# Full matmuls in column tiles, and the third phase of the VectorE exponential added by GpSimd

## The chip, the cores and the metric

The kernel runs on one core of one Trainium2 chip. The metric is the time of one execution in device microseconds (us). All executions of the kernel before lay between 801 and 824 us. They differ mainly in how long TensorE's clock was granted at half speed, which each run records as a mean granted clock. A run counts as slow when it is over 1.5% above the fastest of its kernel, and as fast otherwise.

## The reference, cut to what matters

```python
# S = 2048 tokens, D = 512, 32 heads of 16, F = 1792, all bfloat16
g = sigmoid((x * gate_w).sum(-1, keepdims=True))
a = softmax(q @ k.T * 16**-0.5) @ v  (per head), then @ wo
b = (sigmoid(x @ w_gate) * (x @ w_up)) @ w_down
return g * a + (1 - g) * b
```

The largest part is the exponential of 32 x 2048 x 2048 scores.

## The kernel before

The kernel contains a small scheduler. It describes each instruction as a task with an engine, a planned duration and its inputs, and lays out a fixed order per engine. On the chip each engine runs its order strictly and waits on semaphores. A wrong planned duration makes no wrong result, only an order that doesn't fit.

Scores are computed with keys on the partitions. There are 32 units (8 groups of four heads by 4 blocks of 512 queries), each with 16 key tiles. For twelve key tiles ScalarE computes the exponential. For the other four (1, 5, 9, 13) VectorE does it by a trick: a linear map of the score, written as a 16-bit integer, is the bit pattern of a float16 close to the exponential. Three such patterns, shifted by a third of an octave each and weighted, give a better one. The first shift ("phase") is the map from PSUM; the second and third add a constant to the first, SBUF to SBUF:

```python
PH_OFF = (0, 342, 683)
...
es.append(P.add("dve", 0.61, lambda v, b=b, bp=bp, i=i: v.tensor_scalar(
    PDu[:, bp.slot, 0, i, :], bk(b), EXP_A, EXP_B, op0=ALU.mult, op1=ALU.add), [t], [b, bp], kind="x", prio=1.0))
...
ph_ = [es]
for m in range(1, NPH):
    ph_.append([P.add("dve", 0.33, lambda v, bp=bp, m=m: v.tensor_scalar(
        PDu[:, bp.slot, m, :, :], PDu[:, bp.slot, 0, :, :], float(PH_OFF[m]), None, op0=ALU.add), es, [bp], kind="x")])
```

A block is two heads of one key tile: 1024 elements per partition. There are 256 blocks, and three buffers for them. TensorE works in three modes. Scores use row tiles (32 rows each). PV products (probabilities by values) use four column tiles of 17 columns. Everything else, here called full matmuls, uses the whole array. GpSimd prepares keys and queries and is idle most of the time.

```python
eK[g, r, c] = P.add("pool", 1.0, lambda p, r=r: p.tensor_scalar(
    K[:, g, r, c * 512:(c + 1) * 512], kraw[:, kr.slot, :], msk[:, r:r + 1], msk[:, 2 + r:3 + r],
    op0=ALU.mult, op1=ALU.add), [ev, e_msk], [kr], kind="m")
...
eVm[g, kt, m] = P.add("pool", 0.35, lambda p, i=i, kt=kt, m=m: p.tensor_scalar(
    Vm[:, m - 1, i, 8 * g:8 * g + 8, :], V[:, kt, 8 * g:8 * g + 8, :], PH_W[m], 1.0,
    op0=ALU.mult, op1=ALU.mult), [eV[g, t0], e_one], kind="m", prio=1)
```

## Time and profile before

| | before |
|---|---|
| time, two runs | 801.67 and 812.08 us |
| profiled run | span 817.3 us, mean granted clock 0.964 |
| TensorE, ScalarE, VectorE, GpSimd busy | 94%, 93%, 82%, 11% |

The profiled run was a slow one, with 61 us at half clock. The prediction shows the lines that carry the reading. Three more rows are GpSimd's in the groups of instructions. Columns: line, engine, operation, output and input with shapes and types, count; then busy us and the mean ns of one; then idle time before them.

```profile
L624 POOL TENSOR_SCALAR K<-un,msk 128x512 bf16<-128x512 bf16 x28 | 26.3, 947 | 10.3 <-ACT un L612 10.2
...
L668 POOL COPY Q<-Q 128x512 bf16<-128x512 bf16 x15 | 10.5, 699 | 0.0
L699 POOL TENSOR_SCALAR Vm<-V 128x136 bf16<-128x136 bf16 x32 | 9.9, 309 | 81.8 <-DVE V L695 53.5 <-DVE e2p L718 24.7 <-DVE a_ L636 2.5
```

### The profile page before, as it was taken

The numbers are of one execution on the slowest core, as the hardware profiler recorded it, in microseconds if no ns is written. First come the engines' busy times: TensorE is split into PE (matmuls) and PEld (weight loads), VectorE is DVE, ScalarE is ACT, GpSimd is POOL, SyncE is SP. The second block draws the span as 40 slices with busy tenths as digits, with TensorE's granted clock in tenths as the row PEclk, the third lists the DMA queues.
The fourth block names the chain that finished last, engine by engine and source line by source line (L and its number), as shares of the span: only waits on it lengthen the run. The fifth ranks groups of instructions, "written<-read, shape, count | busy, mean of one in ns | idle before, by whom it ended". The sixth has DMA issues, their size and how long they took to land.

```text
span 817.3 us, 15633 instructions
## 1 busy us (share of the span) xinstructions
PE 770.8 (94%) x6509; PEld 236.6 (29%) x6604; DVE 666.6 (82%) x1318; ACT 756.1 (93%) x838; POOL 88.2 (11%) x160
## 2 busy tenths in 40 slices
PE   7999999999999899999999999999999999999996
PEld 4323333232222222222222222222222222222222
DVE  4986999988988868877889877878988878878783
ACT  3787999989999989999999999999999999999990
POOL 4700523410100000000000001000000100000000
PEclk8975999989999979999999999999999999999998
DMA  9100000011000000000000000000000000000000
GB/s 325 63 2 2 1 2 1 2 57 36 2 1 2 2 1 1 14 8 8 1 2 2 1 1 14 8 8 2 1 1 2 2 14 8 7 1 1 2 1 26
DMA packets 10830, 12.92 MB, mean 16 GB/s; under 512 B 1680, under 2 KB 9736, under 8 KB 10760
## 3 DMA queue, kind: packets, MB, share of 16 engines
q1 hardware_dynamic: 8856, 10.48, 3.8%
q10 hardware_dynamic: 1904, 1.44, 0.5%
q8 instruction: 52, 0.85, 0.4%
q14 instruction: 18, 0.15, 0.1%
HBM read 9.70 MB, written 2.10 MB: 14 GB/s over the span
## 4 chain that ended last, share of the span: by engine, by line
PE 59%; ACT 31%; DVE 7%; issue 1%; DMA 1%; ACTq 0%
ACT PA L786 30%; PE ps_all L753 19%; PE ps_all L762 17%; PE ps_all L596 10%; PE ps_all L858 7%; DVE PD L802 3%; PE ps_all L863 2%; DVE PD L806 2%; PE ps_all L689 1%; ACT tT L730 1%; DMA PD<-in_A_x_dram 1%; PE ps_all L826 1%; PE ps_all L576 1%; PE ps_all L846 0%; DVE hT L733 0%
## 5 line engine op out<-in xcount | busy, mean ns | idle before, releaser
L786 ACT ACTIVATE PA<-ps_all 128x1024 bf16<-128x1024 f32 x768 | 729.4, 1061 | 31.2 <-PE ps_all L753 23.5
L802 DVE TENSOR_SCALAR PD<-ps_all 128x512 uint16<-128x512 f32 x512 | 345.7, 686 | 93.5 <-PE ps_all L753 81.2
L753 PE MATMUL ps_all<-Q,K 32*128 32x512 bf16 x2048 | 312.2, 394 | 22.6 <-ACT PA L786 16.0
L762 PE MATMUL ps_all<-PA,V 128*17 128x512 bf16 x1536 | 244.0, 393 | 0.1
L806 DVE TENSOR_SCALAR PD<-PD 128x1024 uint16<-128x1024 uint16 x512 | 206.7, 437 | 4.8
L762 PE MATMUL ps_all<-PD,Vm 128*17 128x512 f16 x1024 | 183.4, 396 | 1.5 <-issue 1.0
L753 PEld LDWEIGHTS ps_all<-Q,K 32*128 32x128 bf16 x2048 | 75.4, 91 | 274.4 <-ACT PA L786 219.1
L762 PE MATMUL ps_all<-PD,V 128*17 128x512 f16 x512 | 138.2, 394 | 1.1 <-DVE PD L802 0.7
L762 PEld LDWEIGHTS ps_all<-PA,V 128*17 128x17 bf16 x1536 | 51.6, 88 | 59.5 <-issue 50.9
L596 PE MATMUL ps_all<-xT,wu 128*128 128x512 bf16 x208 | 64.8, 388 | 1.5 <-issue 0.8
L596 PE MATMUL ps_all<-xT,wg 128*128 128x512 bf16 x194 | 63.1, 388 | 2.8 <-issue 1.9
L858 PE MATMUL ps_all<-un,hT 128*128 128x512 bf16 x200 | 60.1, 383 | 3.0 <-issue 2.1
L835 POOL TENSOR_TENSOR rs<-rec,e 128x16 f32<-128x16 f32 x32 | 8.0, 250 | 499.1 <-DVE rec L833 498.9
L762 PEld LDWEIGHTS ps_all<-PD,Vm 128*17 128x17 bf16 x1024 | 40.3, 89 | 37.5 <-issue 30.7
L733 DVE SCALAR_TENSOR_TENSOR hT<-tT,ps_all 128x512 bf16<-128x512 bf16 x56 | 38.2, 682 | 12.6 <-PE ps_all L596 12.4
L762 PEld LDWEIGHTS ps_all<-PD,V 128*17 128x17 bf16 x512 | 29.4, 88 | 24.5 <-issue 19.5
L730 ACT ACTIVATE tT<-ps_all 128x512 bf16<-128x512 f32 x56 | 35.5, 634 | 0.0
L666 POOL TENSOR_TENSOR qsq<-Q 128x512 bf16<-128x512 bf16 x15 | 16.5, 1098 | 106.5 <-DVE Q L665 106.5
L624 POOL TENSOR_SCALAR K<-un,msk 128x512 bf16<-128x512 bf16 x28 | 26.3, 947 | 10.3 <-ACT un L612 10.2
L596 PEld LDWEIGHTS ps_all<-xT,wg 128*128 128x128 bf16 x224 | 16.7, 97 | 35.6 <-issue 28.1
L596 PEld LDWEIGHTS ps_all<-xT,wu 128*128 128x128 bf16 x224 | 16.9, 97 | 33.8 <-issue 24.3
L858 PEld LDWEIGHTS ps_all<-un,hT 128*128 128x128 bf16 x224 | 16.9, 97 | 33.4 <-issue 24.8
(79 smaller groups left out, 354.2 us busy)
## 6 DMA issues: line engine op xcount, KB each, us to landing
wg<-in_B_w_gate_dram SPq DMA_DIRECT2D x1, 1792.0 KB, 11.9
wu<-in_B_w_up_dram SPq DMA_DIRECT2D x1, 1792.0 KB, 16.3
un<-in_B_w_down_dram SPq DMA_DIRECT2D x1, 1792.0 KB, 8.6
out_dram<-ost SPq DMA_DIRECT2D x14, 128.0 KB, 1.7
PD<-in_A_x_dram SPq DMA_DIRECT2D x4, 256.0 KB, 6.1
PD<-in_A_x_dram ACTq DMA_DIRECT2D x4, 256.0 KB, 6.9
un<-in_A_wqkv_dram SPq DMA_DIRECT2D x1, 512.0 KB, 8.8
wo<-in_A_wo_dram SPq DMA_DIRECT2D x1, 512.0 KB, 14.9
```

Of the source, the lines that this page charges most:

```text
L596: return lambda pe: pe.matmul(bk(b), w_ap(dt), x_ap(dt), start=(dt == 0), stop=(dt == 3))
L624: eK[g, r, c] = P.add("pool", 1.0, lambda p, r=r: p.tensor_scalar(K[:, g, r, c * 512:(c + 1) * 512], kraw[:, kr.slot, :], msk[:, r:r + 1], ...
L666: s = P.add("pool", 1.15, lambda p: p.tensor_tensor(qsq[:, sq.slot, :], Q[:, bq.slot, 0, :], Q[:, bq.slot, 0, :], ALU.mult), [ev], [sq, bq ...
L730: et = P.add("act", 0.48, lambda a: a.activation(tT[:, t_.slot, :], bk(b), ACTF.Tanh, scale=0.5), [l1], [b, t_], kind="m")
L733: e_h[c, ft] = P.add("dve", 0.62, lambda v: v.scalar_tensor_tensor(hT[:, h_.slot, :], tT[:, t_.slot, :], 1.0, bk(b2), ALU.add, ALU.mult), ...
L753: return pe.matmul(bk(b), K[32 * j:32 * j + 32, g, r, kt * 128:(kt + 1) * 128], Q[32 * j:32 * j + 32, bq.slot, r, :], start=True, stop=Tru ...
L762: return pe.matmul(bk(bpv)[32 * j:32 * j + DH + 1, :], lhs(h), rhs(), start=t.first, stop=t.last, tile_position=(0, 32 * j), skip_group_ch ...
L786: return a.activation(o, ps_all[:, lo:hi + 1:hi - lo, :], ACTF.Exp, bias=ACT_BIAS, scale=SCALE)
L802: es.append(P.add("dve", 0.61, lambda v, b=b, bp=bp, i=i: v.tensor_scalar(PDu[:, bp.slot, 0, i, :], bk(b), EXP_A, EXP_B, op0=ALU.mult, op1 ...
L806: ph_.append([P.add("dve", 0.33, lambda v, bp=bp, m=m: v.tensor_scalar(PDu[:, bp.slot, m, :, :], PDu[:, bp.slot, 0, :, :], float(PH_OFF[m] ...
L858: mms.append((MM, lambda pe, i=i, h_=h_, ft=ft: pe.matmul(bk(b), hT[:, h_.slot, sl], wd[:, ft, :], start=(i == 0), stop=(i == n - 1))))
L863: mms.append((MM, lambda pe, i=i, bs=bs, g=g: pe.matmul(bk(b), OTs[:, bs.slot, sl], wo[:, g, :], start=(i == 0), stop=(i == n - 1))))
```

## The change

The intent: VectorE, at 82%, gives one of three phases to the idle GpSimd. Full matmuls are issued as four column tiles, so that they share PV's mode and need no change of mode beside PV work. The issue rule waits for fuller score sets.

```diff
-N_A, N_D, N_F, N_DF, D_LAG, D_LEAD, N_C = 2, 2, 2, 3, 6, 3, 2
+N_A, N_D, N_F, N_DF, D_LAG, D_LEAD, N_C = 3, 2, 2, 3, 6, 3, 2
+EARLY, LATE = 1.6, 0.9
...
+                if lead < LATE or two or (len(ds) == 2 and lead < EARLY):
+                    if two and not (len(ds) == 2):
+                        s.append(q)
...
-        self._issue([t], now, "F", [[t]])
+        if t.alt:
+            t.emit = t.alt
+        self._issue([t], now, "C" if t.alt else "F", [[t]])
...
+    def full(b, w, x, first, last):
+
+        def four(pe):
+            for j in range(4):
+                i = pe.matmul(bk(b)[32 * j:32 * j + 32, :], w()[:, 32 * j:32 * j + 32], x(), start=first, stop=last,
+                              tile_position=(0, 32 * j), skip_group_check=True)
+            return i
...
-                        ph_.append([P.add("dve", 0.33, lambda v, bp=bp, m=m: v.tensor_scalar(
+                        ph_.append([P.add(*(("pool", 1.45) if m == 2 else ("dve", 0.33)), lambda v, bp=bp, m=m: v.tensor_scalar(
```

More of the change, by code (lines that the diff above doesn't have):

```diff
@@ L82, in pair, with pairs2 @@
         return next((i for i in range(7) if i in at and i + 1 in at), None)
+    def pairs2(self):
+        at = {i for _, i, _ in self.free}
+        i = self.pair()
+        return i is not None and any(j in at and j + 1 in at for j in range(i + 2, 7))
     def take(self, buf, at=None):
@@ L96 @@
     __slots__ = ("eng", "dur", "emit", "deps", "bufs", "kind", "prio", "key", "lanes", "succ", "nd", "seq", "start",
-                 "vis", "ready", "dma", "nbytes", "group", "unit", "war", "known", "val", "n", "first", "last")
+                 "vis", "ready", "dma", "nbytes", "group", "unit", "war", "known", "val", "n", "first", "last", "alt")
     def __init__(self, eng, dur, emit, deps=(), bufs=(), kind="", prio=0.0, key=0.0, lanes=(), dma=False, nbytes=0, n=0):
@@ L106, in __init__ @@
         self.first = self.last = False
+        self.alt = None
 class Plan:
@@ L126, in group @@
         ts = []
-        for i, (dur, emit) in enumerate(mms):
+        for i, (dur, emit, *alt) in enumerate(mms):
             t = self.add("pe", dur, emit, deps if i == 0 else [ts[0]], ([bank] if bank else []) + list(bufs), kind="F", key=key)
+            t.alt = alt[0] if alt else None
             ts.append(t)
@@ L150, in run @@
         self.mode = None
+        self.inflight = []
         self.dma_free = 0.0
@@ L258, in _issue @@
         self.mode = mode
+        if mode == "R":
+            self.inflight = [x for x in self.inflight if x.vis > now] + [x for s in sets for x in s if x.kind == "R"]
         end = t0
@@ L276, in _pe @@
             if p.nd == 0 and ps.pair() is not None and nA < N_A and not (self.dbl and self.dbl[0].n < self.pi - D_LAG):
+                lead = self._lead(now)
                 s = [p]
-                self.pi += 1
-                self.prog = self.pi / len(self.pairs) * UNITS
                 lanes = set(p.lanes)
-                k = 0
-                while k < min(4, len(self.dbl)) and len(s) < 3:
+                q = self.pairs[self.pi + 1] if self.pi + 1 < len(self.pairs) else None
+                two = (q is not None and q.nd == 0 and nA + 2 <= N_A and not lanes & set(q.lanes) and ps.pairs2()
+                       and not (self.dbl and self.dbl[0].n < self.pi + 1 - D_LAG))
+                k, ds = 0, []
+                while k < min(4, len(self.dbl)) and len(ds) < 2:
                     d = self.dbl[k]
-                    if d.n > self.pi + (D_LEAD if len(s) == 1 else -1):
+                    if d.n > self.pi + 1 + (D_LEAD if len(ds) == 0 else -1):
                         break
-                    if (d.nd == 0 and nfree >= 2 + len(s) and nD + len(s) <= N_D and nD + nF + len(s) <= N_DF
+                    if (d.nd == 0 and nfree >= 3 + len(ds) and nD + len(ds) + 1 <= N_D and nD + nF + len(ds) + 1 <= N_DF
                             and d.lanes[0] not in lanes):
-                        s.append(d)
+                        ds.append(k)
                         lanes.add(d.lanes[0])
-                        self.dbl.pop(k)
-                    else:
-                        k += 1
-                return self._issue(s, now, "R", [s])
+                    k += 1
+                if lead < LATE or two or (len(ds) == 2 and lead < EARLY):
+                    if two and not (len(ds) == 2):
+                        s.append(q)
+                    else:
+                        s += [self.dbl[k] for k in ds]
+                        for k in reversed(ds):
+                            self.dbl.pop(k)
+                    self.pi += sum(x.kind == "R" for x in s)
+                    self.prog = self.pi / len(self.pairs) * UNITS
+                    return self._issue(s, now, "R", [s])
         behind = self.dbl and (self.pi >= len(self.pairs) or self.dbl[0].n < self.pi - D_LAG // 2)
@@ L314, in _pe, with _lead @@
         return False
+    def _lead(self, now):
+        x = max(0.0, self.freeat["act"] - now) + sum(t.dur for t in self.ready["act"] if not t.dma)
+        return x + sum(0.905 for t in self.inflight if t.vis > now)
     def _cset(self, now):
@@ L592, in xTd @@
         return [eT[c, 0], eT[c, 1]]
+    def full(b, w, x, first, last):
[4 more added lines that the diff above has]
+            return i
+        return (MM, lambda pe: pe.matmul(bk(b), w(), x(), start=first, stop=last), four)
     def mm4(b, w_ap, x_ap):
-        def one(dt):
-            return lambda pe: pe.matmul(bk(b), w_ap(dt), x_ap(dt), start=(dt == 0), stop=(dt == 3))
-        return [(MM, one(dt)) for dt in range(4)]
+        return [full(b, lambda dt=dt: w_ap(dt), lambda dt=dt: x_ap(dt), dt == 0, dt == 3) for dt in range(4)]
     def xq(c):
@@ L857, in final_mms @@
             h_ = b_h[c, ft]
-            mms.append((MM, lambda pe, i=i, h_=h_, ft=ft: pe.matmul(bk(b), hT[:, h_.slot, sl], wd[:, ft, :], start=(i == 0),
-                                                                    stop=(i == n - 1))))
+            mms.append(full(b, lambda h_=h_: hT[:, h_.slot, sl], lambda ft=ft: wd[:, ft, :], i == 0, i == n - 1))
         for i, g in enumerate(gs_):
@@ L862, in final_mms @@
             i = i + len(fts)
-            mms.append((MM, lambda pe, i=i, bs=bs, g=g: pe.matmul(bk(b), OTs[:, bs.slot, sl], wo[:, g, :], start=(i == 0),
-                                                                  stop=(i == n - 1))))
+            mms.append(full(b, lambda bs=bs: OTs[:, bs.slot, sl], lambda g=g: wo[:, g, :], i == 0, i == n - 1))
         return mms, [e_h[c, ft] for ft in fts] + [e_OTs[c, g] for g in gs_] + [ewo, e_wd], [b_h[c, ft] for ft in fts] + [b_OTs[c, g] for g in gs_]
```

## The prediction

> **What bounds the kernel now.** I read the page first (busy shares and chain), then the groups, the windows by stage, and timelines of ScalarE, TensorE and the VectorE/GpSimd pair.
>
> ```profile
> PE 770.8 (94%) x6509; PEld 236.6 (29%) x6604; DVE 666.6 (82%) x1318; ACT 756.1 (93%) x838; POOL 88.2 (11%) x160
> PE 59%; ACT 31%; DVE 7%; issue 1%; DMA 1%; ACTq 0%
> L786 ACT ACTIVATE PA<-ps_all 128x1024 bf16<-128x1024 f32 x768 | 729.4, 1061 | 31.2 <-PE ps_all L753 23.5
> L802 DVE TENSOR_SCALAR PD<-ps_all 128x512 uint16<-128x512 f32 x512 | 345.7, 686 | 93.5 <-PE ps_all L753 81.2
> L806 DVE TENSOR_SCALAR PD<-PD 128x1024 uint16<-128x1024 uint16 x512 | 206.7, 437 | 4.8
> ```
>
> Two engines are nearly full, and the chain alternates between them. ScalarE has a floor: where it isn't starved it starts an exponential every 0.915 us (a row of three took 2.85 us, a lone one 1.02). 768 of them are 703 us, and 56 tanh at 0.475 us between starts add 27, so 730 us. The first exponential starts at 25.8 us and the last ends at 799.0, so ScalarE loses some 43 us in those 773. The rest of the span, 26 us ahead and 18 us behind, is projections and final matmuls.
>
> TensorE's busy share says little, so I take starts. These rows are of the timeline of TensorE from 664 us on (start, duration, line, operation):
>
> ```profile
> 664.18 0.39 PE L762 MATMUL ps_all<-PD,Vm 128*17 128x512 f16 x1
> ...
> 664.63 0.38 PE L762 MATMUL ps_all<-PA,V 128*17 128x512 bf16 x1
> ...
> 664.94 0.39 PE L753 MATMUL ps_all<-Q,K 32*128 32x512 bf16 x3
> ...
> 665.80 0.39 PE L753 MATMUL ps_all<-Q,K 32*128 32x512 bf16 x3
> ...
> 666.13 0.82 PE L858 MATMUL ps_all<-un,hT 128*128 128x512 bf16 x3
> ...
> 666.88 0.39 PE L753 MATMUL ps_all<-Q,K 32*128 32x512 bf16 x3
> ```
>
> Three sets of four PV matmuls start from 664.18 to 664.63, one per 0.22 us; a score set follows the last of them after 0.31 us, a full matmul follows a score set after 0.33 us. So a set of 512 columns costs 0.216 to 0.221 us in any mode, and a change of mode (row tiles, column tiles, full) adds 0.10 us. Over the whole trace the medians are 0.221 (PV after PV), 0.216 (full after full), and 0.31 to 0.32 for each kind of change. The instruction order of the kernel before has 797 score sets, 799 PV sets, 907 full matmuls of 512 columns, 577 small ones and 1716 changes. From the starts in the trace, sets come to 552 us and changes to 170 us, 722 in all. Of the rest of the span, 21 us are lost in stretches at half clock and about 70 us are waits of TensorE, 5 to 10 us in every 100. So nothing that leaves TensorE's work as it is can win more than part of those 70.
>
> VectorE is third. It holds 7% of the chain, but where it does, GpSimd is often the reason. Rows of the VectorE timeline and the GpSimd timeline:
>
> ```profile
> 217.07 1.60 DVE L806 TENSOR_SCALAR PD<-PD 128x1024 uint16<-128x1024 uint16 x2
> 217.23 1.15 POOL L666 TENSOR_TENSOR qsq<-Q 128x512 bf16<-128x512 bf16 x1 [7.22 <-DVE Q L665]
> ```
>
> Two phase adds usually take 0.75 us; here 1.60, because the second waits until GpSimd's 1.15 us operation has ended. The chain of waits has these 1.51 us on it.
>
> **What the Trainium skill says.**
> - "SBUF — State Buffer", section "Who interferes with whom": a VectorE instruction in a two-port mode and a GpSimd instruction exclude each other for the whole instruction, and the first to start wins. The trace agrees: 436 phase adds with no GpSimd operation beside them average 0.421 us and never exceed 0.429; of the 76 beside one, the worst take 1.26 us.
> - "VectorE: DVE Perf Modes", section "The perf-mode tier table": tensor_scalar from and to SBUF on 16-bit data gets the fastest mode, any PSUM operand loses the two-port modes. So the phase add (SBUF, uint16; 1024 elements in 0.42 us) takes the lock and the first phase (from PSUM; 512 elements in 0.68 us) doesn't. The ratio in the trace fits.
> - "TensorEngine Tiling (Array Packing)", section "Key Properties": changing the tiling mode drains TensorE. The trace shows the drain as 0.10 us.
> - "GPSIMD Engine Reference", section "Engine selection": elementwise work on GpSimd is about 2x slower for two inputs and near line rate for one. For this case the trace says worse, since VectorE has its fast mode: see below.
>
> **The change part by part.**
> *Column tiles.* 864 full matmuls become 864 sets of four with 32 columns each, in PV's mode. A set should cost PV's 0.221 us instead of 0.216: +4 us. What it should bring is fewer changes, since full work may now follow PV work without a drain. I counted the order of the changed kernel: 1583 changes instead of 1716, so 133 x 0.101 = -13.4 us. Most full work sat between two score sets, and score sets are still row tiles: the change there stays.
> *The new issue rule* waits for fuller score sets and allows three pairs of banks. In the order: 813 score sets instead of 797 (+16 x 0.219 = +3.5 us), and only 22 of them with two pairs; 26 were issued with two pairs already in flight. So the third pair is hardly ever used: eight banks less PV's and those of VectorE and full work leave no room. Score sets still wait mostly for the exponential two before (704 of 768).
> *PV sets* are cut up more, since the third phase arrives apart: 838 instead of 799 (+39 x 0.221 = +8.6 us).
> TensorE's sum: +4 - 13.4 + 3.5 + 8.6 = +3 us. The change promises less draining, and the order gives it back in partly filled sets.
> *Third phase to GpSimd.* VectorE loses 256 adds of 0.404 us (206.7/512), 103 us. GpSimd's uncontested tensor_scalar takes 0.30 us for 136 elements and 0.76 us for 512, 1.22 ns an element; for 1024 I estimate 0.76 + 512 x 0.00122 = 1.39 us. 256 x 1.39 = 356 us, with about 0.1 us of waiting each 380, and GpSimd goes from 88 to about 470 us (57%). It fits on average, but from 25 to 50 us and 125 to 150 us GpSimd is already busy for 14.5 and 12.2 us of 25, and eight adds per unit of 24 us want another 11.
> *The lock.* The second and third phase of a block become ready at the same moment. In VectorE's new order the second-phase add comes directly after its block's first phase in 118 of 256 blocks: VectorE wins, GpSimd starts 0.1 us late. In 75 blocks one other operation (0.6 to 0.7 us) comes between: GpSimd has the lock by then, and the add waits some 1.39 + 0.1 - 0.68 = 0.8 us, together 60 us. The other 63 wait 0 to 0.2 us, and neighbouring blocks collide now and then: another 10 to 20 us. So VectorE's saving of 103 us shrinks to about 25 to 35 (about 635 us busy), and its stalls come in lumps of 0.8 us with the next PSUM eviction behind them, so that banks come free late.
> *On the path.* TensorE +3 us. Lock stalls: 75 of 0.8 us, of which I let a fifth reach TensorE's in-order queue, +12. Relief on VectorE: the phase adds hold 1.8% of the chain (15 us), half of it goes, -7; shorter queues ahead of evictions, -6. Sum +2 us on 806.9, so 809.
>
> **The rivals.**
> (a) VectorE's relief counts in full: the lock seldom hits because VectorE often idles before an add (93.5 us before the first phase alone), so collisions spread out. TensorE's waits of 70 us then shrink by 20 to 25: 783 to 788. For it: VectorE is on the chain behind full matmuls and score sets. Against it: 138 of 256 adds are ordered so that GpSimd gets there first.
> (b) GpSimd's latency becomes the wait: the third phase comes 1.5 us after the first instead of 0.8, in-order TensorE stalls on it, above all in the first 175 us where GpSimd also prepares keys and queries. With 0.1 us per block, 25 us: 830. For it: TensorE has no slack, and each stall counts in full. Against it: the order was made with a long third phase in it.
> (c) Column tiles are slower than PV: 32 columns of weights instead of 17, four loads for one. If each set took 0.24 us, 864 x 0.02 = +17 us: 824. Against it: weight loads of 17 and 128 columns take 88 and 97 ns and lie under the 216 ns before them.
> (d) The clock: this profile had 61 us at half clock (21 us lost); the two timed runs are 10 us apart. It may fall either way by 10 us.
>
> **Range and chances.** The centre is 809. (a) and a lucky clock give 785 to 790, (b) or (c) 825 to 830; 8 times in 10 I expect 788 to 830. Faster by over 2% needs less than 791, which only (a) nearly whole reaches: 0.14. Slower by over 2% needs over 823: 0.26. Within 2%: 0.60.
>
> **What would show it.** Right: sets of column-tiled full matmuls start 0.22 us apart; PE waits like before; second-phase adds at 0.6 us or more on average with a tail at 1.2 us or more; GpSimd near 470 us; ScalarE's gaps after the first exponential still near 40 us. Wrong: phase adds still at 0.42 us and VectorE near 570 us (then (a)); a large wait of TensorE for GpSimd's PD (then (b)); column sets over 0.23 us apart (then (c)); ScalarE's exponentials in long rows at 0.92 us, which would mean the new issue rule feeds it better than I counted.

## The result

The changed kernel took 1001.96 us (999.77 and 1004.15). The ratio to before is 1.239, 95% interval 1.215 to 1.262. Ratios here are the mean time of one kernel's fast runs over that of the other's in the same rounds, so not quite the ratio of the medians. The prediction was 809 us, 788 to 830. It was wrong by far more than its range.

The page of the changed kernel, busy times and chain; then its groups:

```profile
PE 859.9 (86%) x9172; PEld 250.5 (25%) x9196; DVE 642.9 (64%) x1062; ACT 776.8 (77%) x838; POOL 814.2 (81%) x416
...
POOL 61%; PE 27%; DVE 10%; issue 1%; DMA 1%; ACT 0%; ACTq 0%
...
L820 ACT ACTIVATE PA<-ps_all 128x1024 bf16<-128x1024 f32 x768 | 746.8, 1029 | 193.7 <-PE ps_all L787 183.9
L840 POOL TENSOR_SCALAR PD<-PD 128x1024 uint16<-128x1024 uint16 x256 | 732.5, 2878 | 145.5 <-DVE PD L836 144.8
L836 DVE TENSOR_SCALAR PD<-ps_all 128x512 uint16<-128x512 f32 x512 | 345.9, 687 | 242.5 <-PE ps_all L787 199.2
...
L840 DVE TENSOR_SCALAR PD<-PD 128x1024 uint16<-128x1024 uint16 x256 | 164.4, 642 | 5.7
```

GpSimd was not on the chain before, and now is 61% of it. Its add takes 2878 ns on average. The 30 that have no VectorE add beside them take 2.76 us, so this is no waiting. The instruction itself is twice my estimate of 1.39 us. ScalarE's idle time before its exponentials went from 31 to 194 us.

The waits show the ring that closes, longest first (engine, what it did, for whom it waited: us in total, times, longest):

```profile
DVE PD L836 <- PE ps_all L787: 199.2, 204, 7.8
ACT PA L820 <- PE ps_all L787: 183.9, 206, 6.2
PEld ps_all L796 <- POOL PD L840: 173.5, 148, 2.8
POOL PD L840 <- DVE PD L836: 144.8, 73, 6.0
...
PE ps_all L796 <- POOL PD L840: 110.8, 119, 2.3
```

TensorE reaches a PV product of the third phase and stands (111 us) until GpSimd has written it. Behind it in the fixed order stand the next scores, so ScalarE (184 us) and VectorE (199 us) have nothing to do. Then GpSimd in turn waits for VectorE's first phase (145 us). One such moment, in the timelines of GpSimd and of TensorE near 601 to 608 us:

```profile
601.44 8.87 POOL L840 TENSOR_SCALAR PD<-PD 128x1024 uint16<-128x1024 uint16 x3 [2.59 <-DVE PD L836]
```

```profile
605.54 0.39 PE L796 MATMUL ps_all<-PD,Vm 128*17 128x512 f16 x3
605.55 0.59 PE L796 MATMUL ps_all<-PA,V 128*17 128x512 bf16 x2
607.48 0.38 PE L796 MATMUL ps_all<-PD,Vm 128*17 128x512 f16 x1 [1.34 <-POOL PD L840]
...
607.80 0.39 PE L787 MATMUL ps_all<-Q,K 32*128 32x512 bf16 x3
```

Three adds take 8.87 us, and TensorE's scores at 607.80 come late by the 1.34 us that the PV product before them waited. TensorE pays a second price: its clock is granted at half speed for 136 us of the trace instead of 61 (mean clock 0.933 against 0.964, though before was a slow run).

The stretches from 40 to 140 us and from 640 to 740 us of the changed kernel (columns: length, then busy us and count of TensorE, its weight loads, VectorE, ScalarE, GpSimd; granted clock; DMA):

```profile
40.00:140.00 100.00, 85.38 (x753) 27.07 (x755) 68.88 (x111) 72.98 (x77) 94.01 (x58) 0.81 0.01 1
640.00:740.00 100.00, 89.18 (x972) 24.18 (x971) 62.25 (x103) 81.61 (x90) 77.96 (x32) 0.93 0.01 3
```

GpSimd is nearly full in the early stretch, where it also prepares keys and queries. Later it is 78% busy and the ring of waits takes the rest.

### The profile page after: what moved, and what is told of

It is laid out like the page before. It is cut to its first block, busy times and chain, and to the rows that moved or that the text cites. A ratio compares the mean times of both kernels' runs of the same rounds, so it can differ in the third digit from the quotient of the medians.

```text
span 1002.4 us, 20903 instructions
## 1 busy us (share of the span) xinstructions
PE 859.9 (86%) x9172; PEld 250.5 (25%) x9196; DVE 642.9 (64%) x1062; ACT 776.8 (77%) x838; POOL 814.2 (81%) x416
## 4 chain that ended last, share of the span: by engine, by line
POOL 61%; PE 27%; DVE 10%; issue 1%; DMA 1%; ACT 0%; ACTq 0%
POOL PD L840 55%; PE ps_all L625 9%; PE ps_all L787 9%; PE ps_all L796 7%; DVE PD L836 6%; POOL K L658 2%; POOL qsq L700 1%; POOL un L654 1%; POOL Q L702 1%; DVE PD L840 1%; DVE hT L767 1%; DMA PD<-in_A_x_dram 1%; PE ps_all L723 1%; DVE OTq L855 0%; POOL Vm L733 0%
## 5 line engine op out<-in xcount | busy, mean ns | idle before, releaser
L840 POOL TENSOR_SCALAR PD<-PD 128x1024 uint16<-128x1024 uint16 x256 | 732.5, 2878 | 145.5 <-DVE PD L836 144.8
L796 PE MATMUL ps_all<-PD,Vm 128*17 128x512 f16 x1024 | 238.4, 402 | 115.7 <-POOL PD L840 110.8
L796 PE MATMUL ps_all<-PA,V 128*17 128x512 bf16 x1536 | 287.2, 404 | 1.0 <-issue 1.0
L840 DVE TENSOR_SCALAR PD<-PD 128x1024 uint16<-128x1024 uint16 x256 | 164.4, 642 | 5.7
L625 PE MATMUL ps_all<-xT,wg 128*32 128x512 bf16 x896 | 85.9, 394 | 0.4 <-DVE hT L767 0.3
L625 PE MATMUL ps_all<-xT,wu 128*32 128x512 bf16 x896 | 81.6, 406 | 0.6 <-DVE PD L836 0.4
L625 PE MATMUL ps_all<-un,hT 128*32 128x512 bf16 x896 | 79.7, 405 | 0.5 <-DVE xT L913 0.5
L855 DVE CAST OTq<-ps_all 128x512 bf16<-128x512 f32 x32 | 22.0, 687 | 21.0 <-PE ps_all L796 21.0
L625 PEld LDWEIGHTS ps_all<-un,hT 128*32 128x32 bf16 x896 | 21.8, 97 | 37.4 <-issue 27.5
L625 PEld LDWEIGHTS ps_all<-xT,wg 128*32 128x32 bf16 x896 | 21.4, 94 | 37.6 <-issue 28.7
```

The costliest lines, as they stand in the source:

```text
L625: i = pe.matmul(bk(b)[32 * j:32 * j + 32, :], w()[:, 32 * j:32 * j + 32], x(), start=first, stop=last, tile_position=(0, 32 * j), skip_gro ...
L796: return pe.matmul(bk(bpv)[32 * j:32 * j + DH + 1, :], lhs(h), rhs(), start=t.first, stop=t.last, tile_position=(0, 32 * j), skip_group_ch ...
L840: ph_.append([P.add(*(("pool", 1.45) if m == 2 else ("dve", 0.33)), lambda v, bp=bp, m=m: v.tensor_scalar(PDu[:, bp.slot, m, :, :], PDu[:, ...
L855: ev = P.add("dve", 0.61, lambda v: v.tensor_copy(OTq[:, bo.slot, :], bk(bpv)), mine, [bpv, bo], kind="m", prio=3)
```

## The experiments

The theory at this point: GpSimd's add alone is the loss, by its length. Rivals: the column tiles or the issue rule do harm too; only the order, planned for 1.45 us, is wrong; the lock between VectorE and GpSimd stretches both. And the length itself needs a cause: the integer type, the size, or something in the instruction.

All kernels gave the right result. The runs of before beside them had medians of 808.6, 809.4 and 811.2 us in the three groups, each on another chip.

### ladder: what does a GpSimd operation cost?

Spare operations on scratch tiles in the kernel before, on GpSimd alone, each four times. Two of the eight probability buffers made room for the tiles; the rest is as before.

```diff
+    zop(lambda g: g.tensor_scalar(fl(zv, U16, 1024), fl(zu, U16, 1024), 683.0, None, op0=ALU.add))
+    zop(lambda g: g.tensor_scalar(fl(zv, BF16, 1024), fl(zu, BF16, 1024), 683.0, None, op0=ALU.add))
...
+    zop(lambda g: g.tensor_scalar(fl(zv, BF16, 1024), fl(zu, BF16, 1024), 683.0, 1.0, op0=ALU.add, op1=ALU.mult))
+    zop(lambda g: g.tensor_tensor(fl(zv, I32), fl(zu, I32), fl(zk, I32), ALU.add))
```

> The kernel before, with a row of spare GpSimd operations (four of each form) put in where GpSimd idles; only their durations count. Theory A (the type): the add of an immediate on uint16 is slow on GpSimd by itself, 2.7 to 2.8 us for 1024 elements in any access pattern and about half for 512, while bfloat16 at 1024 takes 1.0 to 1.4 us, the size of my estimate. Theory B (the length or the pattern): bfloat16 at 1024 also takes 2.7 us or more. Theory C (contention with VectorE): uint16 at 1024 has a minimum well under 2.7 us where VectorE does nothing beside it. An int32 tensor_tensor over the same bytes (512 elements) should take 1.0 to 1.5 us; if it does, it can replace the uint16 add.

Groups of GpSimd instructions of this run:

```profile
L938 POOL TENSOR_SCALAR zv<-zu 128x1024 bf16<-128x1024 bf16 x4 | 11.3, 2819 | 0.3
...
L937 POOL TENSOR_SCALAR zv<-zu 128x1024 uint16<-128x1024 uint16 x4 | 11.1, 2782 | 0.3
...
L940 POOL TENSOR_SCALAR zv<-zu 128x512 bf16<-128x512 bf16 x4 | 6.4, 1588 | 0.2
L943 POOL TENSOR_TENSOR zv<-zu,zk 128x512 int32<-128x512 int32 x4 | 5.2, 1312 | 0.3
L941 POOL TENSOR_SCALAR zv<-zu 128x1024 bf16<-128x1024 bf16 x4 | 4.4, 1090 | 0.2
```

The type is not the cause: bfloat16 takes as long as uint16. Nor is the length or contention: the minimum for uint16 was 2.77 us, and 512 elements take 1.5 to 1.6. By the words of the expectation this is theory B, but the last row says more. The same 1024 bfloat16 elements take 1.09 us when the instruction has two operations, an add and then a multiplication by 1.0. More work takes 2.6 times less time.

### ladder_two: which forms are slow?

The same scaffold, all on uint16 and 1024 elements.

```diff
+    zop(lambda g: g.tensor_scalar(zv[:, :, :], zu[:, :, :], 683.0, None, op0=ALU.add))
+    zop(lambda g: g.tensor_scalar(zv[:, :, :], zu[:, :, :], 683.0, 1.0, op0=ALU.add, op1=ALU.mult))
+    zop(lambda g: g.tensor_scalar(zv[:, :, :], zu[:, :, :], 1.0, 683.0, op0=ALU.mult, op1=ALU.add))
+    zop(lambda g: g.tensor_scalar(zv[:, :, :], zu[:, :, :], 683.0, 0.0, op0=ALU.add, op1=ALU.add))
+    zop(lambda g: g.tensor_scalar(zv[:, :, :], zu[:, :, :], 2.0, None, op0=ALU.mult))
+    zop(lambda g: g.tensor_scalar(zv[:, :, :], zu[:, :, :], 2.0, 1.0, op0=ALU.mult, op1=ALU.mult))
+    zop(lambda g: g.tensor_scalar(zv[:, :, :], zu[:, :, :], 683.0, None, op0=ALU.max))
+    zop(lambda g: g.tensor_copy(zv[:, :, :], zu[:, :, :]))
```

> The kernel before with spare GpSimd operations on uint16, 1024 elements, four of each: add alone; add then multiply by 1; multiply by 1 then add; add then add 0; multiply alone; multiply then multiply; max alone; copy. Theory A1 (one operation alone takes a slow path, whatever it is): the three with one operation take 2.7 to 2.9 us, those with two 1.0 to 1.3 us. A2 (only the add alone is slow): multiply and max alone at 1.0 to 1.3 us. A3 (only bfloat16 has the fast path): all uint16 forms at 2.7 us. The copy should take about 1.0 us in each case.

Its groups, L935 to L942 being the eight lines above in their order:

```profile
L938 POOL TENSOR_SCALAR zv<-zu 128x1024 uint16<-128x1024 uint16 x4 | 14.9, 3726 | 0.3
...
L941 POOL TENSOR_SCALAR zv<-zu 128x1024 uint16<-128x1024 uint16 x4 | 11.6, 2902 | 0.2
L939 POOL TENSOR_SCALAR zv<-zu 128x1024 uint16<-128x1024 uint16 x4 | 11.3, 2821 | 0.2
L935 POOL TENSOR_SCALAR zv<-zu 128x1024 uint16<-128x1024 uint16 x4 | 11.2, 2807 | 0.3
...
L940 POOL TENSOR_SCALAR zv<-zu 128x1024 uint16<-128x1024 uint16 x4 | 4.4, 1098 | 0.2
L942 POOL COPY zv<-zu 128x1024 uint16<-128x1024 uint16 x4 | 4.4, 1093 | 0.2
L937 POOL TENSOR_SCALAR zv<-zu 128x1024 uint16<-128x1024 uint16 x4 | 4.3, 1082 | 0.3
L936 POOL TENSOR_SCALAR zv<-zu 128x1024 uint16<-128x1024 uint16 x4 | 4.3, 1068 | 0.2
```

Any single operation is slow (2.8 to 2.9 us: add L935, multiply L939, max L941). Two operations with a multiplication among them go at the speed of a copy (1.07 to 1.10 us: L936, L937, L940). A1 holds, with an exception that none of the theories had: two adds (L938) are the slowest of all, 3.7 us. So it is not simply "two operations are fast". Some pairs have a fast path, and the runs show three of them. Why, no run here shows.

### col_only: the change without GpSimd

```diff
-                        ph_.append([P.add(*(("pool", 1.45) if m == 2 else ("dve", 0.33)), ...
+                        ph_.append([P.add("dve", 0.33, ...
```

> The changed kernel with the third phase back on VectorE. If GpSimd's third phase is the whole loss, this returns to the level of before: 0.98 to 1.01 of it, that is 790 to 815 us (the order has 1585 changes of mode). If the column tiles or the new issue rule are at fault too, it stays over 1.03.

810.10 us (median of four, one of them slow), ratio 0.997, interval 0.987 to 1.006. Column tiles and the issue rule do no harm by themselves, and bring nothing clear. That rival falls.

### pool_only: GpSimd without the rest

One line of the change, in the kernel before:

```diff
-    ph_.append([P.add("dve", 0.33, lambda v, bp=bp, m=m: v.tensor_scalar(
+    ph_.append([P.add(*(("pool", 1.45) if m == 2 else ("dve", 0.33)), lambda v, bp=bp, m=m: v.tensor_scalar(
```

> The kernel before with only the third phase moved to GpSimd, planned with 1.45 us. If GpSimd's operation is the cause by itself, 1.20 to 1.26 of before (970 to 1015 us), with GpSimd over 800 us busy. If it takes the column tiles or the issue rule to make it hurt, under 1.10.

1002.66 us, ratio 1.237, GpSimd busy 813 us. The whole loss comes with this one line.

### pool_long: the same work, planned with its real length

```diff
-                        ph_.append([P.add(*(("pool", 1.45) if m == 2 else ("dve", 0.33)), ...
+                        ph_.append([P.add(*(("pool", 2.9) if m == 2 else ("dve", 0.33)), ...
```

> The changed kernel with the third phase planned at 2.9 us, what it measured, instead of 1.45. If the loss is GpSimd's throughput (256 adds of 2.76 us and 83 us of other work are 790 us, plus some 25 us before the first), the time falls but stays bound by GpSimd: 850 to 930 us. If it was the plan's wrong order alone, it comes to 800 to 830 us. If the order doesn't matter, it stays at about 1000.

898.07 us, ratio 1.107. Its page:

```profile
PE 848.2 (95%) x9175; PEld 266.3 (30%) x9196; DVE 646.0 (72%) x1062; ACT 759.6 (85%) x838; POOL 805.5 (90%) x416
...
PE 59%; ACT 16%; DVE 14%; POOL 8%; DMA 1%; issue 1%; ACTq 0%; DVEq 0%
```

So the loss of 195 us (1002 less 807) has two parts. About 104 (1002 less 898) come from an order made for 1.45 us when the add takes 2.76 to 2.88. About 90 remain when the order knows the length. The expectation said GpSimd would then be the bound. At 90% busy it is close to full, but it holds only 8% of the chain. TensorE holds 59% and hardly waits for GpSimd (its matmuls for 1.6 us, its weight loads for 4.6). Its starts show more, smaller sets: 878 groups of scores, by my count, against 790 before and 809 in the changed kernel. Counted in the orders that the kernels lay out when built, this one has 916 score sets and 993 PV sets where the changed kernel has 813 and 838. At 0.22 us each, the 258 more come to 57 us, an estimate; this trace also has 75 us at half clock, pool_two's 18. So the cut-up sets can be most of the 90 us. How these divide between GpSimd's pace and the sets, no run tells apart.

### pool_two: the changed kernel with another form of the add

The instruction order on every engine is that of the changed kernel. Only the form of 256 instructions differs, and the result is the same:

```diff
-    PDu[:, bp.slot, m, :, :], PDu[:, bp.slot, 0, :, :], float(PH_OFF[m]), None, op0=ALU.add), es, [bp], kind="x")
+    PDu[:, bp.slot, m, :, :], PDu[:, bp.slot, 0, :, :], float(PH_OFF[m]), 1.0, op0=ALU.add, op1=ALU.mult), es, [bp], kind="x")
```

> The changed kernel, its order on every engine untouched, with the GpSimd add written with two operations (add the phase, then multiply by 1.0) instead of one. The first ladder had the two-operation form at 1.09 us where the one-operation form took 2.77 to 2.82. Theory A (the form of that one instruction is the whole loss): GpSimd's adds take 1.05 to 1.3 us, GpSimd is busy 350 to 420 us, TensorE's wait for GpSimd nearly vanishes, and the time comes to what the prediction said for the rest, 795 to 815 us, 0.98 to 1.01 of before. Theory B (with any long third phase on GpSimd the lock against VectorE's adds costs, too): still 1.02 or more of before, with VectorE's second-phase adds at 0.6 us and more. If the form is fast for bfloat16 only, it stays at 1000 us.

804.25 us (four runs), ratio 0.996, interval 0.988 to 1.005. Two rows of its groups:

```profile
L841 POOL TENSOR_SCALAR PD<-PD 128x1024 uint16<-128x1024 uint16 x256 | 306.5, 1198 | 348.2 <-DVE PD L836 343.6 <-DVE gw L741 2.5 <-DVE a_ L670 1.2
...
L845 DVE TENSOR_SCALAR PD<-PD 128x1024 uint16<-128x1024 uint16 x256 | 143.4, 560 | 5.7
```

This settles it: a multiplication by 1.0 takes away 198 us. GpSimd is busy 391 us (49%) instead of 814, and TensorE's matmuls wait for it for 0.6 us (111 us in the changed kernel), its weight loads for 1.5 us instead of 174. Part of the 198 us is the clock, which was at half speed for 18 us instead of 136: at most half of these 118 us, 59 us, by an estimate. The lock is there and is small. Undisturbed adds on GpSimd take 1.04 us, the upper half 1.28, behind a VectorE add; 78 of VectorE's 256 adds are lengthened, by 35 us in all.

### pool_i32: a third way to add

The same bytes as int32 pairs, added to a constant tile with 683 in both halves.

```diff
+    ph_.append([P.add("pool", 1.2, lambda g, bp=bp: g.tensor_tensor(
+        pd32(bp, 2), pd32(bp, 0), k32, ALU.add), es + [e_k32], [bp], kind="x")])
```

> The changed kernel with the third phase on GpSimd as an int32 tensor_tensor add of a constant tile over the same bytes (512 pairs), 1.31 us in the first ladder, planned at 1.2. Theory A: about as pool_two, 795 to 820 us, since the time depends on GpSimd's duration and not on the instruction. If tensor_tensor holds VectorE up in another way, over 1.02 of before.

812.89 us, ratio 1.007, interval 0.997 to 1.017; the add took 1.43 us on average. As the theory wants, another instruction with a short duration repairs the time too. (It was planned at 1.2 us, so its order is not quite that of the changed kernel.)

### pool_two_before: the quick form in the kernel before

```diff
+    if m == 2:
+        ph_.append([P.add("pool", 1.45, lambda v, bp=bp, m=m: v.tensor_scalar(
+            PDu[:, bp.slot, m, :, :], PDu[:, bp.slot, 0, :, :], float(PH_OFF[m]), 1.0, op0=ALU.add, op1=ALU.mult), es, [bp], kind="x")])
+        continue
```

> The kernel before (full matmuls in the full array, old issue rule) with the third phase on GpSimd in the two-operation form. Theory A: 0.98 to 1.01 of before, as pool_two. If the column tiles are what pays, this one is slower than pool_two by over 1%.

817.57 us, ratio 1.013, interval 1.005 to 1.022, against 804.25 for pool_two in the same rounds: 1.7% apart. Here the column tiles with their issue rule do pay, and moving the third phase alone costs: its run at a clock of 0.993 took 816.46 us, the two of before at 0.993 took 801.67 and 801.73. TensorE's starts show one term: 170 us of changes of mode here against 156 in pool_two. They also show 76 us of waits at full clock against 54 (counted as in the prediction), but most of this difference is not real. The trace here lacks the records of 100 matmuls (PE x6504 on the page, its weight loads x6604), that of pool_two 24 (x9172, x9196), and a missing one is counted as 0.22 us of waiting, 22 and 5 us in all.

### pool_two_again and pool_two_first: is there a gain?

pool_two_again is pool_two with more rounds. pool_two_first plans the add at 1.2 us and lets VectorE do its second-phase add before other ready work:

```diff
-    ... float(PH_OFF[m]), None, op0=ALU.add), es, [bp], kind="x")])
+    ... float(PH_OFF[m]), None, op0=ALU.add), es, [bp], kind="x", prio=3.0)])
```

> The two-operation version once more, with more rounds, to see whether the 0.9964 of three rounds is a gain. Since TensorE's sets and changes of mode are as in the changed kernel and cost what they cost before, I expect 0.990 to 1.002 of before, no gain of 2%.

> The two-operation version with the GpSimd add planned at 1.2 us and VectorE's second-phase add put first among what is ready on VectorE, so that VectorE takes the shared port before GpSimd more often (126 of 256 blocks directly after the first phase instead of 118, 93 with one operation between instead of 75). If the 35 us by which the lock lengthens VectorE's adds reach the end, this gains up to 1% on the version without; if VectorE's stalls are hidden behind TensorE and ScalarE, it is the same within 0.5%.

pool_two_again took 802.31 us, ratio 0.989, interval 0.984 to 0.993, just under the 0.990 expected at the least; pool_two_first 812.63, ratio 1.001, interval 0.996 to 1.006. So pool_two is ahead of before by about 1% in these rounds, clear of noise, where the first three rounds could not tell.

The gain goes with the clock. It was 0.991 to 0.998 in the six runs of pool_two_again, and 0.964 to 0.986 in the eleven of before beside them. The time of before follows the clock in all its 25 runs of the experiments: 816.70 us at 0.966, 808.91 to 809.73 at 0.979, 801.67 and 801.73 at 0.993. At 0.994 pool_two_again took 803.79 and 804.02, and pool_two, on the chip of the last two, 802.75 at 0.995. So at equal clock it is no faster than before. Why its clock is higher, no run shows.

The second order is 1.2% worse, against both of its expectations. Its clock was lower too, 0.984 to 0.990. At 0.988 it took 812.05 and 812.28 us, where pool_two took 808.30, so about 4 of the 10 us are left at equal clock. The lock lengthened VectorE's adds by 43 us in it instead of 35, and the order has 15 more changes of mode. What makes the 4 us stays open.

## Why the prediction was wrong, point by point

**The step that failed** is the estimate of GpSimd's duration: "GpSimd's uncontested tensor_scalar takes 0.30 us for 136 elements and 0.76 us for 512, 1.22 ns an element; for 1024 I estimate 0.76 + 512 x 0.00122 = 1.39 us". It measured 2.76 us undisturbed and 2.88 on average. The extrapolation in length was fair. What it took for granted was that the two rows and the new instruction are the same operation because the profile calls all three TENSOR_SCALAR. The rows carry two operations with a multiplication each; the add carries one. In the quick form 1024 elements take 1.04 us, below my estimate. The planned 1.45 us of the scheduler was wrong in the same way.

From there the terms built on it fell. "About 470 us (57%)" became 814. "It fits on average" became a ring of waits. Of the rivals, (b), GpSimd's latency becomes the wait, is what happened in kind. I sized it from the same 1.39 us, hence 25 us instead of 195. The chance of slower, 0.26, came from there.

**What held.**
- Column-tiled full matmuls start 0.216 us after one another or after a PV set in the changed kernel's trace, and a PV set 0.226 us after them (medians); I had 0.221. Changes of mode still cost 0.10 us. Rival (c) is out.
- "The change promises less draining, and the order gives it back": col_only, 0.997 of before.
- The lock: in the changed kernel, second-phase adds took 642 ns on average, up to 1.31 us, as said ("0.6 us or more on average with a tail at 1.2 us or more"). That is in part luck, as GpSimd's adds were twice as long as I had assumed. In pool_two the average was 560 ns. GpSimd had started first at 71 of them, close to my 75, but these grew by 0.44 us each, not 0.8: its quick add is 0.35 us shorter than my 1.39. In all they were lengthened by 35 us, not the 60 and 10 to 20 that I had, and VectorE was busy 614 us instead of my 635.
- The sum for the rest, roughly: with adds of 1.20 us on average (pool_two) and 1.43 us (pool_i32), on both sides of my 1.39, the time was 802 to 804 and 813 us against my 809. That its terms for the path were right is not shown. Rival (a), 783 to 788, did not come either.

**A reading that was off.** I took about 70 us of the span for waits of TensorE. The page has x6509 matmuls and x6604 weight loads, so 95 matmul records are missing, and my sum took the 0.22 us of each for waiting: 21 us. The waits were nearer 50 us, and rival (a) had less to win.

**On the skill.** "SBUF — State Buffer", section "Who interferes with whom", has a VectorE instruction in a two-port mode and a GpSimd instruction exclude each other for the whole instruction. With the quick form the trace agrees: of 70 VectorE adds in pool_two that started while GpSimd's add ran (over 0.06 us after its start), 69 ended after it, by 0.28 us at the median. With the slow form it doesn't. Of 191 such adds in the changed kernel, 113 ended inside GpSimd's add, 63 of them at under 0.45 us. One is in VectorE's timeline, while the first of the three adds shown above ran from 601.44 to 604.70 us:

```profile
603.38 0.43 DVE L840 TENSOR_SCALAR PD<-PD 128x1024 uint16<-128x1024 uint16 x1
```

Those that started in the first 0.5 us of GpSimd's add took 0.97 us on average, those at 1.0 to 1.5 us 0.42, and those at 2.0 to 2.25 us 1.05. So the exclusion lapses in the middle of the slow add, as if it ran in two parts; that it does is a guess.

The page "GPSIMD Engine Reference", section "Engine selection", has one-input work at roughly line rate. That holds for the copy (1.09 us for 1024 elements) and the quick forms, and misleads for the single add (2.77).

## What to carry to other kernels

A duration read from the profile belongs to the whole instruction, its number and kind of operations included, not to the name that the row prints. Before moving work to another engine on an extrapolated cost, put a few spare copies of the exact instruction into an idle stretch and measure it. In a kernel with a fixed order an underestimated duration is paid twice, in the instruction itself and in the order made from it, which here was about half of the 195 us. Before a per cent is credited to a new order, compare the clocks that the runs were granted.

## What the Trainium skill lacked or had wrong

- "GPSIMD Engine Reference", sections "Engine selection" and "Elementwise — side-by-side cycle accounting": they give no cost by form of tensor_scalar. Measured, 1024 16-bit elements: one operation (add, multiply or max with an immediate) 2.78 to 2.90 us on average; add then multiply, multiply then add, multiply then multiply 1.07 to 1.10 us; add then add 3.73 us; copy 1.09 us. The type (uint16, bfloat16, float16) made no difference to the single add.
- The same page's "roughly line-rate" for one input is wrong for the single-operation form: 2.77 us on GpSimd against 0.42 us on VectorE for this add.
- The same page has an exact wrapping int32 tensor_tensor add, but no time for it: 1.26 to 1.33 us for 512 pairs in the ladder. The result was right.
- No page has that a VectorE add can run inside a GpSimd instruction: 63 adds of under 0.45 us did, inside the single-operation form of 2.76 us or more.
- "TensorEngine Tiling (Array Packing)", "Performance Considerations", presents column tiling for small matrices only. No page has that a full matmul of 512 columns may be cut into four column tiles at no cost in their spacing: 0.216 us from set to set, as in the full array.
